# Second layer with its shared partial sum copied from PSUM to PSUM, and the weight splits of the first layer queued later

## The chip, the cores and the metric

One core of a Trainium2 chip runs the whole program. The metric is the device time of the program in microseconds. The kernel before takes 1782.92 us (median of 3 runs, 1781.92 to 1786.9).

## The reference

An attention with keys and values pooled by 8 feeds two layers, each a pair of matrix products over 4608 tokens with a model width of 512 and an inner width of 2048, all in fp32:

```python
def _moe2_ref(x, w_in, w_out):          # the second layer
    h = x @ w_in                        # 4608x512 @ 512x2048
    g = h - np.tanh(h)
    return g @ w_out                    # 4608x2048 @ 2048x512
```

The first layer has the same shape, with `g = ((clip(h, -1, 1) + 1) / 2) ** 2` joined to `h` above 1 in the place of `h - tanh(h)`.

## The kernel before

**The first layer** (lines 572 to 861) goes over 12 blocks of 384 tokens, and in each over 16 slices of the inner width: one *step* is the 12 matmuls of `h_mm`, the 12 of `out_mm` of two steps before, and the elementwise work between them. A dictionary `plan` says what else each step issues. Its slot "ev" holds the copies of the attention's PSUM tiles (`at_evac`, `kv_k_evac`), its slot "w" the preparation of the second layer's weights, one slice `f` in eight steps: `w2_conv` rebuilds fp32 numbers (lines 158 to 165), `w2_sums` forms four sums on POOL (243 to 251), `w2_own` and `w2_mixed` split each number into a high and a low part (`w2_halves`: line 254 on ACT, line 255 on DVE) and send them to DRAM (`w2_place`, line 260, from SP's queue). In this layer the order of an engine's instructions isn't that of the text: a scheduler places them by when it expects their inputs. A block `tc.issue_after(i)` adds that what it holds comes after instruction `i` on that engine.

**The second layer** (lines 868 to 1212) does each 2x2 block product with 7 products instead of 8 (Winograd's form). Tokens go in five groups `J` of 768, 1024, 1024, 1024 and 768; `half(J)` is 384 or 512. For each pair of 128-wide inner slices `q` (8 for each J, 40 in all) there are 7 `h_prod`, each of 6 matmuls of 128 x `half`, onto three PSUM banks A, X and Z. For two pairs together, `k = q // 2` (20 in all), there are 7 `o_prod` of 24 (or 18) matmuls of 256 columns, onto two PSUM tiles of two banks, bo0 and bo1. PE's order is written out by hand: two `h_prod`, one `o_prod`, and so on, with the `o_prod` eight places behind; the first 20 `h_prod` and the last `o_prod` stand alone. All engines run in the order of due times that a planner gives (`at_time`), so a late instruction holds up everything behind it on its engine.

The products share sums. Product 1 is in all four blocks of h, products 1 + 6 are in three. Before the change this is done outside PSUM: ACT copies product 1 out (`v_s`), DVE adds it to bank X after products 6, 5 and 3 (`v_w`, `v_t`, `v_c12`), DVE adds two more (`v_c22`, in SBUF, and `v_c21`), and ACT copies c11 out. Two tanh of 128 x 2 x half on ACT (`v_th`) read these blocks in SBUF, and two subtractions follow (`v_sub`), one on DVE and one on POOL. POOL then forms the sums for the second product (`g_s1` to `g_s4`), ACT and DVE split each operand into high and low (`sp_hi`, `sp_lo`), and after each `o_prod` its PSUM tile is added into one of six sums in SBUF (`add_up`), which `fold` joins on POOL at the end of a J.

At the end of a J the next group's x is loaded, split into 7 operands (`xc_hi` on ACT, `xc_lo` on DVE), with four differences between them on POOL (`x_t1` to `x_t4`). This stretch is called a *switch* below; there are four.

Of the kernel before, what the change touches and what calls it, by code (L numbers as in the profile page):

```python
# [51 lines left out]
def attention_two_moe_kernel(  # L52
# [767 lines left out]
    for f in range(FC):  # L820
# [44 lines left out]
    for x in (ps_a, ps_h, ps_o):  # L865
# [11 lines left out]
        "q0 q1 q2 q3 q4 r3 p1664 o0 o1 g0 s0 q7 q8 p2048 x1 x6 r4 o2 o3 q5 q6 g1 k0 k1 th s1 p1024"  # L877
        " r0 r1 r2 z0 p1728 aS aX a11 a12 a21 a22 u1 u2 x7 x2 x5 x4 x3"
# [5 lines left out]
    for x, n in (("bo0", 2), ("bo1", 2), ("bA", 1), ("bX", 1), ("bZ", 1)):  # L884
        TAGS[x] = one_pool(f"two_{x}", space=PSUM, reuse_waits="tile")
# [4 lines left out]
    HORD = (1, 6, 7, 2, 5, 4, 3)  # L890
# [13 lines left out]
    def wo_load(i):  # L904
        k, m = divmod(i, 7)
        t = WO2[i] = two(f"o{i % NO}", [P, 2, 2, 256], F32R, "wo")
        nc.sync.dma_start(out=t.bitcast(F32), in_=w2o[k % NGR][:, OSLOT[OORD[m]]])
# [17 lines left out]

    def xc_tile(J, m):
        x = two(f"x{m}", [P, 2, 2, M2], F32R, "xc")
        XC[(J, m)] = x[:, :, :, 0 : half(J)]
# [29 lines left out]

    def h_prod(i):
        q, mi = divmod(i, 7)  # L960
        m, J = HORD[mi], q // NPR
        bank = {1: "A", 2: "A", 6: "X", 5: "X", 3: "X", 7: "Z", 4: "Z"}[m]
        new = m in (1, 6, 7)
        if new:
            BK[(q, bank)] = two(f"b{bank}", [P, M2], F32, f"bk{bank}")[:, 0 : half(J)]
        o, x, w = BK[(q, bank)], XC[(J, m)], WQ.pop(i).rearrange("p h (c f) -> p h c f", f=P)
# [8 lines left out]
    def g_of(q, i, th=None):  # L975
# [3 lines left out]
        n2 = half(k // NGR)  # L979
        return GR[k][:, p, i, :, 0:n2] if th is None else GR[k][:, p, i, th, 0:n2]  # L980

    def snap(q, name, bank):
        s = SN[(q, name)] = two(name, [P, M2], F32, name)[:, 0 : half(q // NPR)]
        nc.scalar.activation(s, BK[(q, bank)], AF.Copy)

    def v_s(q):
        snap(q, f"s{q % 2}", "A")
# [4 lines left out]
    def s_of(q):  # L992
        return SN[(q, f"s{q % 2}")]

    def v_c11(q):
        nc.scalar.activation(g_of(q, 0, 0), BK.pop((q, "A")), AF.Copy)

    def v_w(q):
        nc.vector.tensor_tensor(g_of(q, 1, 0), BK[(q, "X")], s_of(q), ALU.add)

    def v_t(q):
        nc.vector.tensor_tensor(g_of(q, 1, 1), BK[(q, "X")], s_of(q), ALU.add)  # L1002

    def v_c22(q):
        o = g_of(q, 1, 1)
        nc.vector.tensor_tensor(o, o, SN.pop((q, "z0")), ALU.add)  # L1006

    def v_c21(q):
        o = g_of(q, 1, 0)
        nc.vector.tensor_tensor(o, BK.pop((q, "Z")), o, ALU.add)  # L1010

    def v_c12(q):
        nc.vector.tensor_tensor(g_of(q, 0, 1), BK.pop((q, "X")), SN.pop((q, f"s{q % 2}")), ALU.add)  # L1013

    def v_th(q, i):
# [46 lines left out]

    def o_prod(n):
        k, mi = divmod(n, 7)
        m, n2 = OORD[mi], half(k // NGR)
        new = m in (1, 6, 7)
        chain = {1: 0, 2: 0, 7: 1, 4: 1, 6: 2, 5: 2, 3: 2}[m]
        if new:
            OB[(k, chain)] = two(f"bo{(k + (chain == 2)) % 2}", [P, 4, 256], F32, "ob")
        o, x, w = OB[(k, chain)], SP2.pop(n), WO2.pop(n)  # L1070
        nch = n2 // P
# [19 lines left out]

    def add_up(n):
        k, mi = divmod(n, 7)
        m, J, g = OORD[mi], k // NGR, k % NGR
        name = {1: "S", 2: "11", 6: "X", 5: "22", 3: "12", 7: "22", 4: "21"}[m]
        chain = {1: 0, 2: 0, 7: 1, 4: 1, 6: 2, 5: 2, 3: 2}[m]
        o = OB[(k, chain)][:, 0 : half(J) // P]
        a = ac_of(J, name)
        if g == 0 and m != 7:
# [3 lines left out]
        if g == NGR - 1:  # L1103
            if m == 2:
                y_out(J, 0, 0, "11")
            if m == 7:
                y_out(J, 1, 1, "22")
            if m == 3:
                y_out(J, 0, 1, "12")
            if m == 4:  # L1110
                y_out(J, 1, 0, "21")

    def fold(J, name, by):
        a = ac_of(J, name)
        nc.gpsimd.tensor_tensor(a, a, ac_of(J, by), ALU.add)
# [32 lines left out]
    seq += late_o[3:] + [("o", n) for n in range(7 * NG - LAG, 7 * NG)]  # L1148
# [13 lines left out]
    for n in range(7 * NG):  # L1162
        at_time((-26, -25, -54, -0.5)[n] if n < NO else began[n - NO] + 3, wo_load, n)
        k, mi = divmod(n, 7)
        r = half(k // NGR) / M2
        t = max(began[n] - 6.6 * r, split_at(n))
        at_time(t, sp_hi, n)
        at_time(t + 1.1 * r, sp_lo, n)
    for q in range(2 * NG):
        e = {m: ended[7 * q + i] for i, m in enumerate(HORD)}  # L1170
        at_time(e[1] + 0.05, v_s, q)
        at_time(e[6] + 0.1, v_w, q)
        at_time(e[7] + 0.05, v_z, q)
# [70 lines left out]
```

## Time and profile before

| | |
|---|---|
| median of 3 runs | 1782.92 us |
| the profiled execution | 1787.46 us |
| its span, first to last instruction | 1785.6 us |
| PE busy in the span | 1699.8 us (95%) |
| DVE, ACT, POOL busy | 1214.3, 880.1, 695.2 us |
| first matmul of the second layer | at 1002.43 us of the span |
| mean granted TensorE clock | 0.986 of full speed |

The profile counts an engine as busy from an instruction's start to its end. Matmuls overlap, so a product of six matmuls is best read from the start of one product to the start of the next. "Idle before, releaser" is the time for which an engine had nothing running, and the instruction whose end let it go on. [...]

### The profile page before, as it was taken

Reading aid. Unit: us, or ns where it says so; the run is one execution under the profiler, and the core shown is the slowest. Engines: PE = TensorE matmul, PEld = TensorE weight load, DVE = VectorE, ACT = ScalarE, POOL = GpSimd, SP = SyncE. Lnnn points to the kernel's source line nnn. Section 1 sums busy time; section 2 is a strip of 40 time slices with the busy share of each in tenths; the row PEclk is TensorE's granted clock in tenths of the full one; section 3 lists DMA queues with packets and bytes.
Section 4 is the critical chain, followed back from the end, with each engine's and each line's share of the span. In section 5 each row is a group of like instructions: output and inputs, shape, how many; then the busy total and the mean of one; then the engine's idle time right before and its main releaser. Section 6 shows DMA issues by size and latency. Waiting matters only on the chain. (4 is left out here: it accounts for less than half of the span.)

```text
span 1785.6 us, 28158 instructions
## 1 busy us (share of the span) xinstructions
PE 1699.8 (95%) x10176; PEld 1586.3 (89%) x10176; DVE 1214.3 (68%) x1685; ACT 880.1 (49%) x1962; POOL 695.2 (39%) x585
## 2 busy tenths in 40 slices
PE   7999999999999999999999999899999989998996
PEld 6569989899999999998999998799889978998996
DVE  7876676666666566765545558857975797578676
ACT  5656665556555565555444354343434434433442
POOL 5441243321443223431000245543663465456342
PEclk9999999999999999999999999999999999998999
DMA  7641144424433343433111577577556756664864
GB/s 221 231 135 30 56 126 117 154 61 126 134 106 121 89 130 88 145 98 98 28 66 54 171 244 264 165 224 231 161 185 205 234 165 206 198 210 153 280 214 138
DMA packets 220218, 270.56 MB, mean 152 GB/s; under 512 B 82672, under 2 KB 151792, under 8 KB 220080
## 3 DMA queue, kind: packets, MB, share of 16 engines
q1 hardware_dynamic: 219824, 267.98, 48.3%
q8 instruction: 81, 1.33, 0.3%
q0 software_dynamic: 256, 0.79, 0.1%
q14 instruction: 57, 0.47, 0.1%
HBM read 219.94 MB, written 48.23 MB: 150 GB/s over the span
## 5 line engine op out<-in xcount | busy, mean ns | idle before, releaser
L1078 PEld LDWEIGHTS ob<-wo,sp 128*128 128x128 f32 x3024 | 385.8, 194 | 35.8 <-DVE sp L1061 17.7
L1078 PE MATMUL ob<-wo,sp 128*128 128x256 f32 x3024 | 392.5, 286 | 25.0 <-DVE sp L1061 15.7
L602 ACT ACTIVATE g<-g,half 128x384 f32<-128x384 f32 x192 | 118.7, 618 | 183.5 <-DVE g L598 181.6
L591 PE MATMUL ph<-xh,whl 128*128 128x384 f32 x704 | 197.0, 340 | 0.6 <-DVE g L606 0.6
L636 PE MATMUL po<-gh,whl 128*128 128x384 f32 x704 | 196.6, 340 | 0.0
L1021 POOL TENSOR_TENSOR g<-g,th 128x1024 f32<-128x1024 f32 (+1 forms) x40 | 90.8, 2271 | 260.2 <-ACT th L1017 168.7
L970 PE MATMUL bkX<-xc,wq 128*128 128x512 f32 (+1 forms) x720 | 175.9, 380 | 15.9 <-DVE g L1013 11.1
L479 POOL TENSOR_TENSOR ex<-ex,rc 128x432 f32<-128x432 f32 x44 | 41.7, 948 | 350.9 <-ACT g L602 176.8
L1017 ACT ACTIVATE th<-g 128x1024 f32<-128x1024 f32 (+1 forms) x80 | 78.0, 975 | 201.9 <-DVE g L1010 116.7
L1061 DVE TENSOR_TENSOR sp<-g,sp 128x1024 fp32r<-128x1024 f32 (+1 forms) x100 | 149.5, 1495 | 30.5 <-ACT sp L1056 30.4
L615 DVE TENSOR_TENSOR gl<-g,gh 128x384 fp32r<-128x384 f32 x176 | 109.1, 620 | 88.3 <-ACT gh L614 87.3
L970 PEld LDWEIGHTS bkX<-xc,wq 128*128 128x128 f32 x720 | 131.1, 192 | 35.2 <-DVE g L1013 12.6
L606 DVE TENSOR_TENSOR g<-ph,g 128x384 f32<-128x384 f32 x192 | 106.6, 555 | 65.3 <-ACT g L602 63.3
L598 DVE TENSOR_SCALAR g<-ph 128x384 f32<-128x384 f32 x192 | 105.6, 550 | 57.3 <-PE ph L591 51.9
L1102 DVE TENSOR_TENSOR ac<-ob,ac 128x1024 f32<-128x1024 f32 (+1 forms) x110 | 122.0, 1110 | 31.0 <-PE ob L1078 30.8
L1056 ACT ACTIVATE sp<-g 128x1024 fp32r<-128x1024 f32 (+1 forms) x100 | 97.0, 970 | 81.3 <-PE ob L1078 52.0
L614 ACT ACTIVATE gh<-g 128x384 fp32r<-128x384 f32 x176 | 91.8, 522 | 89.4 <-DVE g L606 51.8
L591 PEld LDWEIGHTS ph<-xh,whl 128*128 128x128 f32 x704 | 128.5, 188 | 1.9 <-DVE g L606 1.6
L636 PEld LDWEIGHTS po<-gh,whl 128*128 128x128 f32 x704 | 128.7, 188 | 0.0
L636 PE MATMUL po<-gh,wh 128*128 128x384 f32 x352 | 122.3, 347 | 0.0
L591 PE MATMUL ph<-xh,wh 128*128 128x384 f32 x352 | 121.2, 344 | 0.2 <-DVE g L606 0.2
L328 POOL TENSOR_TENSOR kvraw<-kvraw 128x768 f32<-128x768 f32 (+2 forms) x84 | 111.1, 1322 | 23.0 <-DMA kvraw<-in_v_dram 16.4
(175 smaller groups left out, 3895.7 us busy)
## 6 DMA issues: line engine op xcount, KB each, us to landing
wq<-w2c SPq DMA_DIRECT2D x280, 256.0 KB, 3.6
wo<-w2o SPq DMA_DIRECT2D x140, 512.0 KB, 3.6
wraw<-in_moe_w_in_dram SPq DMA_DIRECT2D x32, 512.0 KB, 3.9
wraw<-in_moe_w_out_dram SPq DMA_DIRECT2D x32, 512.0 KB, 5.0
out_dram<-ac SPq DMA_DIRECT2D x72, 128.0 KB, 1.8
x2d<-ost SPq DMA_DIRECT2D x44, 192.0 KB, 1.9
w2c<-wraw SPq DMA_DIRECT2D x16, 512.0 KB, 2.8
w2o<-wraw SPq DMA_DIRECT2D x16, 512.0 KB, 2.8
```

Of the source, the lines that this page charges most:

```text
L328: eng.tensor_tensor(a[..., 0:n], a[..., 0:n], a[..., n : 2 * n], ALU.add)
L591: nc.tensor.matmul(ps, a[:, cs], x[:, c, :], start=(i == 0), stop=(i == 3 * KC - 1))
L598: nc.vector.tensor_scalar(a, hp[t], -1.0, 1.0, ALU.max, ALU.min)
L602: nc.scalar.activation(a, a, AF.Square, bias=half, scale=0.5)
L606: nc.vector.tensor_tensor(a, hp.pop(t), a, ALU.max)
L615: nc.vector.tensor_tensor(gl, a, gh.bitcast(F32), ALU.subtract)
L636: nc.tensor.matmul(o, a, m, start=(f == 0 and i == 0), stop=(f == FC - 1 and i == len(ops) - 1))
L970: nc.tensor.matmul(o, w[:, wi, c], x[:, xi, c], start=new and n == 0, stop=n == 5, skip_group_check=not new)
L1056: nc.scalar.activation(x[:, 0, :, 0 : half(k // NGR)], o_src(k, OORD[mi]), AF.Copy)
L1061: nc.vector.tensor_tensor(x[:, 1], o_src(k, OORD[mi]), x[:, 0].bitcast(F32), ALU.subtract)
L1078: nc.tensor.matmul(o[:, c], x[:, xi, p, c * P : (c + 1) * P], w[:, p, wi], start=new and first, stop=True, skip_group_check=not (new and f ...
L1102: nc.vector.tensor_tensor(a, o, a, ALU.add)
```

## The change

In the first layer, `w2_sums` is issued one step earlier, and `w2_own` and `w2_mixed` go through `behind`, which puts their ACT and DVE instructions after the newest one of the text on the same engine.

In the second layer, ACT copies product 1 from bank A into bank X (`v_seed`), and products 6, 5 and 3 accumulate onto it there. ACT takes one copy of 1 + 6 out of X (`v_u`), and DVE writes c21 in place in bank Z and c22 into a new bank Y, the second half of a tile that it shares with A. The four tanh read PSUM, one block each, and the four subtractions are all on DVE, from PSUM into SBUF. `o_prod` does likewise: ACT copies product 1's tile into the tile of products 6, 5 and 3 (`o_seed`), so four output sums remain, and `fold` is gone. `open_x` and `fill` are a few matmuls that open a bank ahead of the first copy into it. Products 6 and 7 change places. The operands of x rotate through eight buffers instead of seven, and their due times move forward. The last eight `o_prod` change their order.

```diff
+    def behind(fn, *a):
+        with tc.issue_after(newest(E.Activation)), tc.issue_after(newest(E.DVE)):
+            fn(*a)
...
-        add(t + 4, "w", w2_sums, f)
-        add(t + 5, "w", w2_own, f)
-        add(t + 6, "w", w2_mixed, f)
+        add(t + 3, "w", w2_sums, f)
+        add(t + 5, "w", behind, w2_own, f)
+        add(t + 6, "w", behind, w2_mixed, f)
...
-    for x, n in (("bo0", 2), ("bo1", 2), ("bA", 1), ("bX", 1), ("bZ", 1)):
+    for x, n in (("bo0", 2), ("bo1", 2), ("bA", 2), ("bX", 1), ("bZ", 1)):
...
-    HORD = (1, 6, 7, 2, 5, 4, 3)
+    HORD = (1, 7, 6, 2, 5, 4, 3)
...
+    def fill(o, w):
+        for i in range(0, o.shape[1], M2):
+            nc.tensor.matmul(o[:, i : i + M2], w[:, 0:P], w, start=True, stop=True)
...
+    def v_seed(q):
+        nc.scalar.activation(new_bank(q, "X"), bank(q, "A"), AF.Copy)
...
-    def v_w(q):
-        nc.vector.tensor_tensor(g_of(q, 1, 0), BK[(q, "X")], s_of(q), ALU.add)
-
-    def v_t(q):
-        nc.vector.tensor_tensor(g_of(q, 1, 1), BK[(q, "X")], s_of(q), ALU.add)
+    def v_u(q):
+        snap(q, f"s{q % 2}", "X")
 
     def v_c22(q):
-        o = g_of(q, 1, 1)
-        nc.vector.tensor_tensor(o, o, SN.pop((q, "z0")), ALU.add)
+        nc.vector.tensor_tensor(bank(q, "Y"), bank(q, "X"), SN.pop((q, "z0")), ALU.add)
...
+    def v_c21(q):
+        o = bank(q, "Z")
+        nc.vector.tensor_tensor(o, o, SN.pop((q, f"s{q % 2}")), ALU.add)
...
+    def v_th(q, b):
+        th = SN[(q, b)] = two(f"t{next(n_th) % 2}", [P, M2], F32, "th")[:, 0 : half(q // NPR)]
+        nc.scalar.activation(th, bank(q, b), AF.Tanh)
+
+    def v_sub(q, b):
+        nc.vector.tensor_tensor(g_of(q, *WHERE[b]), BK.pop((q, b)), SN.pop((q, b)), ALU.subtract)
...
+    def o_seed(k):
+        o = OB[(k, 2)] = two(chain_bank(k, 2), [P, 4, 256], F32, "ob")
+        c = half(k // NGR) // P
+        nc.scalar.activation(o[:, 0:c], OB[(k, 0)][:, 0:c], AF.Copy)
...
-        if g == 0 and m != 7:
+        if g == 0 and m not in (7, 4):
             nc.scalar.activation(a, o, AF.Copy)
         else:
             nc.vector.tensor_tensor(a, o, a, ALU.add)
...
-    def fold(J, name, by):
-        a = ac_of(J, name)
-        nc.gpsimd.tensor_tensor(a, a, ac_of(J, by), ALU.add)
...
-    seq += late_o[3:] + [("o", n) for n in range(7 * NG - LAG, 7 * NG)]
+    end = [("o", n) for n in range(7 * NG - LAG, 7 * NG)]
+    seq += late_o[3:] + [end[i] for i in (1, 0, 3, 2, 5, 4, 7, 6)]
...
+        at_time(e[1] + 0.05, v_seed, q)
         at_time(e[7] + 0.05, v_z, q)
+        at_time(e[6] + 0.05, v_u, q)
+        at_time(e[2] + 0.1, v_th, q, "A")
+        at_time(e[2] + 0.9, v_sub, q, "A")
+        at_time(e[5] + 0.05, v_c22, q)
+        at_time(e[5] + 0.9, v_th, q, "Y")
+        at_time(e[5] + 1.6, v_sub, q, "Y")
         at_time(e[4] + 0.05, v_c21, q)
+        at_time(e[4] + 0.9, v_th, q, "Z")
+        at_time(e[4] + 1.6, v_sub, q, "Z")
+        at_time(e[3] + 0.05, v_th, q, "X")
+        at_time(e[3] + 0.8, v_sub, q, "X")
...
-        lo = {1: 2.6, 6: 10.6, 2: 12.6, 7: 15.6, 5: 21.6, 4: 25.6, 3: 29.6}
...
+                t = max(free, min(ended[last] + (-8, 4, 8, 10.5, 15, 19, 23)[i], due))
```

`e[m]` is the planned end of product `m` of pair `q`, and `ended[last]` that of the first product of a J's last pair.

## Rows read from the trace of the kernel before

**Rows 1.** Windows of layer two: stretch, length, busy PE PEld DVE ACT POOL, clock, DMA.

```profile
1100.00:1155.00 55.00, 44.64 (x259) 38.47 (x258) 48.85 (x41) 21.19 (x27) 31.86 (x13) 0.97 0.55 168
1155.00:1265.00 110.00, 110.00 (x697) 99.52 (x697) 74.06 (x67) 47.42 (x54) 55.29 (x20) 1.00 0.70 221
1265.00:1325.00 60.00, 51.76 (x307) 45.81 (x307) 51.77 (x40) 23.57 (x27) 35.04 (x13) 0.94 0.51 153
...
1435.00:1490.00 55.00, 46.70 (x275) 41.28 (x274) 47.25 (x35) 21.46 (x25) 35.79 (x13) 0.94 0.52 158
...
1615.00:1670.00 55.00, 48.30 (x319) 47.69 (x318) 45.19 (x37) 19.32 (x26) 36.85 (x14) 0.91 0.58 190
...
1742.00:1785.60 43.60, 30.14 (x223) 28.72 (x222) 28.71 (x31) 9.91 (x12) 11.10 (x5) 0.96 0.44 133
```

**Rows 2.** Waits of PE in 1000:1790: total us, times, longest us.

```profile
PE ob L1078 <- DVE sp L1061: 15.7, 10, 2.7
PE bkX L970 <- DVE g L1013: 11.1, 5, 4.4
```

**Rows 3.** Timeline of DVE around the second switch: start, us, instruction.

```profile
1283.84 2.83 DVE L1061 TENSOR_TENSOR sp<-g,sp 128x1024 fp32r<-128x1024 f32 x1
...
1301.89 3.41 DVE L1021 TENSOR_TENSOR g<-g,th 128x1024 f32<-128x1024 f32 x1
...
1318.01 1.22 DVE L1061 TENSOR_TENSOR sp<-g,sp 128x1024 fp32r<-128x1024 f32 x1
```

**Rows 4.** Timeline of POOL over the same stretch.

```profile
1282.31 3.27 POOL L1035 TENSOR_TENSOR u<-g 128x1024 f32<-128x1024 f32 x1
...
1295.69 8.52 POOL L1115 TENSOR_TENSOR ac<-ac 128x1024 f32<-128x1024 f32 x3 [3.43 <-DVE ac L1102]
```

**Rows 5.** Three lines of DVE, whole run: duration ns min/median/max, first and last start.

```profile
L1006 DVE TENSOR_TENSOR g<-g,z x40: 551/684/2760, 1008.5 to 1742.5; 128x512 f32<-128x512 f32 x24, 128x384 f32<-128x384 f32 x16
...
L1013 DVE TENSOR_TENSOR g<-bkX,s x40: 543/678/693, 1010.0 to 1743.4; 128x512 f32<-128x512 f32 x24, 128x384 f32<-128x384 f32 x16
...
L1102 DVE TENSOR_TENSOR ac<-ob,ac x110: 943/1211/1225, 1043.7 to 1780.8; 128x1024 f32<-128x1024 f32 x66, 128x768 f32<-128x768 f32 x44
```

**Rows 6.** The same for ACT's copy out of bank Z.

```profile
L984 ACT ACTIVATE z<-bkZ x40: 472/598/602, 1005.8 to 1736.8; 128x512 f32<-128x512 f32 x24, 128x384 f32<-128x384 f32 x16
```

**Rows 7.** Windows of layer one, two stretches and the sum over 240:1000.

```profile
495.00:600.00 105.00, 97.83 (x573) 93.81 (x572) 66.06 (x119) 57.67 (x169) 41.06 (x61) 0.98 0.42 127
...
735.00:840.00 105.00, 99.34 (x566) 95.53 (x565) 66.76 (x121) 58.33 (x169) 39.06 (x55) 0.95 0.36 109
...
sum 760.00, PE 737.86 PEld 722.22 DVE 468.32 ACT 411.70 POOL 210.66; mean PE 73.79 PEld 72.22 DVE 46.83 ACT 41.17 POOL 21.07
```

**Rows 8.** Waits of PE in 240:840.

```profile
PE psc L450 <- ACT kt L377: 7.1, 7, 2.0
PE ppv L548 <- DVE al L530: 6.5, 5, 2.6
PE ppv L551 <- DVE al L530: 3.9, 3, 1.3
```

**Rows 9.** Timelines of ACT and of DVE around one weight split, 255:268.

```profile
258.96 1.06 ACT L254 ACTIVATE wraw<-wf 128x1024 fp32r<-128x1024 f32 x1 [0.44 <-DVE wf L165]
...
261.87 1.23 DVE L255 TENSOR_TENSOR wf<-wf,wraw 128x1024 fp32r<-128x1024 f32 x1 [2.13 <-POOL wraw L246]
```

**Rows 10.** Timeline of PE around the second switch and in the last stretch.

```profile
1277.95 3.04 PE L1078 MATMUL ob<-wo,sp 128*128 128x256 f32 x24
1280.83 1.57 PE L970 MATMUL bkZ<-xc,wq 128*128 128x512 f32 x6
1282.24 1.56 PE L970 MATMUL bkA<-xc,wq 128*128 128x512 f32 x6
...
1749.09 2.39 PE L1078 MATMUL ob<-wo,sp 128*128 128x256 f32 x18 [1.60 <-ACT th L1017]
```

**Rows 11.** ACT's wait for the next slice's weights, whole run.

```profile
ACT wraw L158 <- DMA wraw<-in_moe_w_out_dram: 13.9, 10, 3.8
```

More of the change, by code (lines that the diff above doesn't have):

```diff
@@ L957, in x_t4, with bank, new_bank @@
         x_eng(J).tensor_tensor(XR[(J, 1)], XR[(J, 1)], x_src(J, 6), ALU.subtract)
+    BANK = {1: "A", 2: "A", 6: "X", 5: "X", 3: "X", 7: "Z", 4: "Z"}
+    def bank(q, b):
+        return BK[(q, b)]
+    def new_bank(q, b):
+        if b == "A":
+            t = two("bA", [P, 4, 256], F32, "bkA").rearrange("p c f -> p (c f)")
+            BK[(q, "Y")] = t[:, M2 : M2 + half(q // NPR)]
+        else:
+            t = two(f"b{b}", [P, M2], F32, f"bk{b}")
+        o = BK[(q, b)] = t[:, 0 : half(q // NPR)]
+        return o
     def h_prod(i):
@@ L961, in h_prod @@
         m, J = HORD[mi], q // NPR
[L962 to L966, printed above, removed]
+        new = m in (1, 7)
+        o = new_bank(q, BANK[m]) if new else bank(q, BANK[m])
+        x, w = XC[(J, m)], WQ.pop(i).rearrange("p h (c f) -> p h c f", f=P)
         n = 0
@@ L973, in h_prod, with open_x, g_of @@
                 n += 1
-    def g_of(q, i, th=None):
+    def fill(o, w):
+        for i in range(0, o.shape[1], M2):
+            nc.tensor.matmul(o[:, i : i + M2], w[:, 0:P], w, start=True, stop=True)
+    def open_x():
+        fill(two("bX", [P, M2], F32, "bkX"), WQ[0].rearrange("p h f -> p (h f)"))
+    def g_of(q, i, th):
         k, p = divmod(q, 2)
@@ L1061, in sp_lo, with chain_bank @@
         nc.vector.tensor_tensor(x[:, 1], o_src(k, OORD[mi]), x[:, 0].bitcast(F32), ALU.subtract)
+    W1 = {}
+    CHAIN = {1: 0, 2: 0, 7: 1, 4: 1, 6: 2, 5: 2, 3: 2}
+    def chain_bank(k, chain):
+        if k == NG - 1 and chain == 0:
+            return "bA"
+        return f"bo{(k + (chain == 2) + (k == NG - 1)) % 2}"
     def o_prod(n):
@@ L1065, in o_prod @@
         m, n2 = OORD[mi], half(k // NGR)
-        new = m in (1, 6, 7)
-        chain = {1: 0, 2: 0, 7: 1, 4: 1, 6: 2, 5: 2, 3: 2}[m]
+        new, chain = m in (1, 7), CHAIN[m]
         if new:
-            OB[(k, chain)] = two(f"bo{(k + (chain == 2)) % 2}", [P, 4, 256], F32, "ob")
+            OB[(k, chain)] = two(chain_bank(k, chain), [P, 4, 256], F32, "ob")
         o, x, w = OB[(k, chain)], SP2.pop(n), WO2.pop(n)
+        if m == 1:
+            W1[k] = w
         nch = n2 // P
@@ L1094, in add_up @@
         m, J, g = OORD[mi], k // NGR, k % NGR
-        name = {1: "S", 2: "11", 6: "X", 5: "22", 3: "12", 7: "22", 4: "21"}[m]
-        chain = {1: 0, 2: 0, 7: 1, 4: 1, 6: 2, 5: 2, 3: 2}[m]
-        o = OB[(k, chain)][:, 0 : half(J) // P]
+        if m == 1:
+            if k in (0, NGR):
+                b = two(chain_bank(k, 2), [P, 4, 256], F32, "ob").rearrange("p c f -> p (c f)")
+                fill(b, W1.pop(k)[:, 0].rearrange("p h f -> p (h f)"))
+            o_seed(k)
+            return
+        name = {2: "11", 6: "21", 5: "22", 3: "12", 7: "22", 4: "21"}[m]
+        o = OB[(k, CHAIN[m])][:, 0 : half(J) // P]
         a = ac_of(J, name)
-        if g == 0 and m != 7:
+        if g == 0 and m not in (7, 4):
             nc.scalar.activation(a, o, AF.Copy)
@@ L1102, in add_up @@
             nc.vector.tensor_tensor(a, o, a, ALU.add)
[L1103 to L1111, printed above, removed]
-    def fold(J, name, by):
-        a = ac_of(J, name)
-        nc.gpsimd.tensor_tensor(a, a, ac_of(J, by), ALU.add)
+        if g == NGR - 1 and m in (2, 5 if k == NG - 1 else 7, 3, 4):
+            y_out(J, int(name[0]) - 1, int(name[1]) - 1, name)
     def y_out(J, th, dh, name):
@@ L1147, in attention_two_moe_kernel @@
         seq.insert(len(seq) - 10 + 4 * i - i, x)
-    seq += late_o[3:] + [("o", n) for n in range(7 * NG - LAG, 7 * NG)]
+    end = [("o", n) for n in range(7 * NG - LAG, 7 * NG)]
+    seq += late_o[3:] + [end[i] for i in (1, 0, 3, 2, 5, 4, 7, 6)]
+    ordo = [i for kind, i in seq if kind == "o"]
+    POS = {n: i for i, n in enumerate(ordo)}
     for kind, i in seq:
```

73 lines of the change are left out of this document (27 added, 46 removed).

## The prediction, made before any run of the changed kernel

> **What bounds the kernel now.** I read the windows by stretch first, then PE's waits, then the timelines around them. In layer two PE is busy without a gap between the switches (110.00 of 110.00 us in 1155:1265 [rows 1]), so there no other engine's saving is worth anything. What can be saved lies in five places. [...] The last stretch has 13.5 us without PE, of which about 5 lie behind the last product (the last sum starts at 1780.8 [rows 5], and then its DMA), and 0.04 of 43.6 us by the clock: 8.6 + 1.7 = 10.3 us.
>
> What PE waits for there is DVE: 15.7 us for the low halves of `o_prod`'s operands, and 11.1 us for the sum (`v_c12`) that frees bank X [rows 2]. At the switches DVE is busy 48.9 of 55, 51.8 of 60, 47.3 of 55 and 45.2 of 55 us; between them, 74.1 of 110 [rows 1]. Part of this isn't work. A low half takes 1.22 us alone, but 2.83 us while POOL's `g_s1` runs beside it; DVE's subtraction took 3.41 us beside POOL's folds and what followed them [rows 3, 4]. The sum in SBUF, `v_c22`, has a median of 684 ns and a longest of 2760; the sums with one input in PSUM never go over 693 (512 columns) and 1225 (1024) [rows 5], although POOL ran beside many of them. So an addition of two SBUF tensors slows down beside POOL, one with a PSUM input doesn't.
>
> In layer one PE idles 22.1 us between 240 and 1000 [rows 7], and 17.5 us of its waits are for the attention's copies out of PSUM, `kt` and `al` [rows 8]; the clock of 0.98 and 0.95 in two stretches of 105 us adds 7.4 us [rows 7]. The timeline shows how: a weight split's high half (1.06 us) stands ahead of the copies on ACT, and its low half stands on DVE for 2.13 us until POOL has finished `w2_sums`, which read what it overwrites [rows 9].
>
> **The change, part by part.** *DVE at a switch.* For each pair, five sums of 0.69 us and a subtraction of 1.22 (this is L1102's median as well [rows 5]) become two sums and four subtractions of 0.69 us, all with a PSUM input: 4.67 becomes 4.14 us, and a switch of some 50 us holds 2.5 pairs, 1.3 us. The sum of product 1 (1.21 us [rows 5]) goes once in such a stretch. The first split of x moves from 2.6 us behind the switch to 8 us ahead of it, 1.2 us by [rows 3]'s alone value. POOL loses a subtraction for each pair and four folds for each J; three folds alone took 8.52 us [rows 4], so with the fourth and two or three subtractions about 17 of its 35 busy us [rows 1] are gone. The excess of DVE's instructions with two SBUF inputs over their lone times is what goes with it. In [rows 3] it is 1.6 us for the low half and 2.2 for the subtraction; `v_c22` and the subtraction also leave the kind that is slowed. Taking 2.2 us for the subtraction, 2.1 for one `v_c22` (its longest less its median), and half of 1.6 for each of four low halves gives 7.5 us. DVE gains about 1.3 + 1.2 + 1.2 + 7.5 = 11 us where PE idles 6.7 to 10.4. The relief is as large as the stall, so I expect most of it gone, and with the gaps the stretches at half clock. What is late next is the first low half behind the switch: it stands behind two splits of x while `g_s1` and `g_s2` run, and has some 2 us to spare. I keep 9 of 47.1 us for that: **-38 us**. Bounds: -47 (nothing left) and -24 (half: if the contention with `g_s1` to `g_s4` and `x_t1` to `x_t4`, which stay, is the larger part).
>
> *New waits of PE.* Four chains now pass through two or three engines before a bank is free. For A and Y: `v_c22`, tanh, subtraction, then product 1 of the next pair. Three instructions at 0.69, 0.60 [rows 6] and 0.69, and an allowance of 0.1 for each hand-over, are 2.3 us. Behind product 5 stand products 4 and 3, 1.41 us each, and always an `o_prod` of 2.88 [rows 10]: 5.7 us. X (tanh, subtraction, `v_seed`) and Z have the same 5.7, and `v_seed` itself (0.6 to 0.9 us; the trace shows no write to PSUM but PE's, the copy in [rows 6] is nearest and I take its 0.6) has product 7 and an `o_prod`, 4.3 us. All are covered by about 3.4 us of slack while DVE isn't late: cost nothing. Behind a waiting seed ACT would hold the next `sp_hi`, and PE the rest of its list. At the start of layer two no `o_prod` lies between: two products at three quarters of 1.41 us give 2.1 us against 0.75 of 2.3 plus `v_c21` ahead in DVE's queue, about 2.2. I take 0.3 us for each of two or three pairs, and under 1 us for the few matmuls of `fill`: **+1.5 us** (0 to 4).
>
> `o_seed` has two `h_prod` of cover (2.8 us for a copy of about 1.1), and in the tail the new order puts two other `o_prod` between. PE gets no more matmuls elsewhere. ACT has seven copies and tanh of 0.6 us for a pair in the place of three and two of twice the size, 0.1 to 0.4 us more; it is busy 47.4 of 110 us in the steady stretch [rows 1], so that is hidden.
>
> In this trace a 512-column sum costs DVE the same from PSUM as from SBUF, 678 and 684 ns in the median [rows 5]. [...]
>
> *The tail.* The first stall there waits for a tanh ahead of POOL's subtraction [rows 10]. Now the subtractions are on DVE block by block, so product 1's operand is ready before the last `h_prod` ends; the folds, beside which low halves were slow, are gone; one sum less is made. But `sp_hi` of a product still waits for the buffer of the second one before, with DVE's `g_s1` to `g_s4` in the queue: about a fifth of a product late at several places. **-5.5 us** of 10.3 (-2 to -8).
>
> *Weight splits.* High and low halves now follow the copies of the attention, and `w2_sums`, a step earlier, are done before. The waits of 17.5 us [rows 8] less one of 2.0 in which ACT stood at a weight load, and the 7.4 us of clock, are 22.9 us at stake. The 32 splits still take 1.06 and 1.23 us each on ACT and DVE, only elsewhere, so I take a bit over half: **-13 us** (0 to -22). What the later place costs: SP's `w2_place` moves with it, and so does the load of the next slice into the same buffer, for which ACT already waits 13.9 us [rows 11].
>
> **The sum.** -38 + 1.5 - 5.5 - 13 = -55 us. The profiled execution took 1787.46 us (span 1785.6 and 1.9 around it), 4.5 over the median; 1787.5 - 55 is 1732.5 for such an execution, and 1782.9 - 55 = **1728 us** for the median.
>
> **The rivals.** *All of it* (0.13): every gap at the switches goes, 8 us in the tail, 22 in layer one: -77, 1706 us. For it: 11 us of relief against 6.7 to 10.4.
> *Half* (0.18): DVE is still the later one at the switches (-24), the splits only move the stall (0), tail -2, start +3: -23, 1760 us. For it: `g_s1` to `g_s4` stay on POOL and meet the splits of x.
> *The next weights come late* (0.05): with mixed splits in their planned step, the load has two steps; ACT stands at line 158 as in its longest waits, 2 us for each of 15 slices, all passed on to PE: +30 for -13, so -12, 1771 us. Against it: layer two's weights are complete long before they are read.
> *Slower: the bank chain* (0.06). At product 1 of a pair PE waits for `v_c22`, tanh and subtraction if DVE's queue is more than 3.4 us late in ordinary stretches; each us beyond that costs 40 us over 40 pairs. With 1.8 us beyond (72 us) against -55, 1800 us; it decides from 1.4 us on. For it: waits for the same kind of sum reach 4.4 us at the switches [rows 2]. Against it: between them PE never waits, with a DVE two thirds busy.
> *It doesn't act* (0.03): PE's waits are set by something that the profile names wrongly, such as the weights' DMA; then within 0.3% of 1783.
>
> **How the numbers follow.** The forecast (0.55, some 14 us to either side by its bounds) is 1728. The range has to hold 8 in 10: it goes a little past the middle of the first rival to 1702, and past that of the second to 1766, so that it takes in about three quarters of each (0.10 and 0.14) beside the forecast, 0.79. A measurement of this kernel can tell about 0.3%, 5 us. Faster by more: 0.55 + 0.13 + 0.18 + 0.05 = 0.91; within: 0.03; slower: 0.06.
>
> **What would show it.** Right: in the windows around the four switches PE idles under 3 us each at a clock of 0.98 or more; POOL's busy time falls by over 100 us, with 40 subtractions and 20 folds gone; DVE's subtractions take 0.7 us and the low halves are rarely over 2 us; `kt` and `al` cost PE under 8 us. Wrong: PE's waits name bank A or X behind a subtraction or a seed away from the switches, or ACT's wait for the weights grows; or the switches keep their gaps although DVE is free, in which case another queue set them.

## The result, and the profile after

| | before | after |
|---|---|---|
| median, same chip | 1784.91 us (4 runs, 1781.92 to 1787.47) | 1714.34 us (4 runs, 1711.2 to 1715.59) |
| ratio | | 0.9603, 95% interval 0.958 to 0.9625 |
| span of the profiled execution | 1785.6 us | 1709.3 us |
| first matmul onto bank A (end of layer one) | 1002.4 | 982.2 |
| first to last matmul onto bank A | 737.3 | 686.5 |
| from there to the end of the span | 45.9 | 40.6 |

The change saves 70.6 us by the medians and 76.3 by the two profiled spans, of which 20.2 lie in layer one, 50.8 between the first and the last matmul onto bank A (this stretch holds the four switches), and 5.3 in the tail. The profiled execution of before is the longest of its four and that of after the shortest, which is why the spans give more than the medians; part of the 20.2 is that (see the experiments). The three stretches come from two rows: the span, and the first and last start of the matmuls onto A. After (profile of that tile; duration min/median/max in ns, then first and last start):

```profile
core 0 of [0], span 1709.3 us
...
L992 PE MATMUL bkA<-xc,wq x480: 331/392/499, 982.2 to 1668.7; 128*128 128x512 f32 x96, 128*128 128x384 f32 x64
```

The page of after, busy time, share of the span and instructions: POOL is 155 us less busy than the 695.2 of before, DVE 89 less, ACT 9 more, and PE is busy 98% of the span.

```profile
PE 1673.2 (98%) x10181; PEld 1571.8 (92%) x10181; DVE 1125.5 (66%) x1675; ACT 889.2 (52%) x2052; POOL 539.8 (32%) x525
```

Windows of after at the four switches, each beginning 2 to 5 us ahead of the first low half of the new x (columns as in [rows 1]), and their sum. Against the 10.4, 8.2, 8.3 and 6.7 us of [rows 1], PE idles 0.5 us in the first and nothing in the others, and the granted clock is 1.00 in all four.

```profile
1060.00:1115.00 55.00, 54.54 (x355) 51.07 (x354) 44.27 (x49) 29.28 (x45) 23.04 (x10) 1.00 0.75 234
1205.00:1265.00 60.00, 60.00 (x378) 53.88 (x377) 50.21 (x44) 31.14 (x42) 27.13 (x10) 1.00 0.60 180
1365.00:1420.00 55.00, 55.00 (x352) 49.62 (x351) 47.70 (x43) 29.57 (x39) 25.62 (x10) 1.00 0.64 191
1525.00:1580.00 55.00, 55.00 (x379) 52.37 (x378) 42.69 (x44) 27.98 (x41) 22.73 (x9) 1.00 0.63 193
sum 225.00, PE 224.54 PEld 206.94 DVE 184.88 ACT 117.97 POOL 98.53; mean PE 56.13 PEld 51.74 DVE 46.22 ACT 29.49 POOL 24.63
```

The same four stretches of before, begun 6 to 10 us ahead of the same low half, in sum. PE idles 31.4 us of 225 (one gap of 2.2 us at the third switch lies behind the window; [rows 1] has 33.6). The thing to keep for later is that DVE is busy 208.6.

```profile
sum 225.00, PE 193.65 PEld 175.02 DVE 208.60 ACT 91.12 POOL 152.21; mean PE 48.41 PEld 43.75 DVE 52.15 ACT 22.78 POOL 38.05
```

Over the whole stretch from the first to the last matmul onto A, PE's idle time falls from 36.4 to 0.5 us, and its busy time for the same matmuls from 700.9 to 686.0, at a mean granted clock of 0.98 before and 1.00 after (before, it is 0.50 in 1287:1290, right behind a gap of 2.69 us; after, it is 1.00 at every switch). These are the 50.8 us: 35.9 and 14.9.

[rows 2] leaves out what PE waited for at the first switch of before. In 1090:1145 it is mostly the splits of x, 6.4 us of 10.4:

```profile
PE bkZ L970 <- DVE xc L941: 3.5, 2, 2.0
PE bkX L970 <- DVE xc L941: 2.3, 1, 2.3
...
PE bkZ L970 <- ACT xc L937: 0.6, 1, 0.6
```

PE's waits of after in 1000:1710 (total, times, longest). They answer to [rows 2]: nothing waits for a sum that frees a bank, and low halves cost 0.5 us in the place of 15.7 (once, at the first switch). The other four lines are waits in the tail.

```profile
PE ob L1104 <- ACT ob L1121: 1.6, 1, 1.6
PE ob L1104 <- ACT sp L1073: 1.6, 1, 1.6
PE ob L1104 <- DMA wo<-w2o: 1.1, 1, 1.1
PE ob L1104 <- issue: 0.9, 2, 0.7
PE ob L1104 <- DVE sp L1078: 0.5, 1, 0.5
```

The new instructions, whole run (L1024 is `v_c22`, L1038 a subtraction, L1011 `v_seed`, L1035 a tanh; they answer to [rows 5, 6]): each takes what the prediction gave it, 0.58 to 0.70 us.

```profile
L1024 DVE TENSOR_TENSOR bkA<-bkX,z x40: 566/699/700, 988.0 to 1670.4; 128x512 f32<-128x512 f32 x24, 128x384 f32<-128x384 f32 x16
...
L1038 DVE TENSOR_TENSOR g<-bkA,th x80: 541/679/693, 987.3 to 1672.2; 128x512 f32<-128x512 f32 x48, 128x384 f32<-128x384 f32 x32
...
L1011 ACT ACTIVATE bkX<-bkA x40: 475/582/592, 983.4 to 1663.8; 128x512 f32<-128x512 f32 x24, 128x384 f32<-128x384 f32 x16
...
L1035 ACT ACTIVATE th<-bkA x80: 478/597/601, 986.8 to 1671.0; 128x512 f32<-128x512 f32 x48, 128x384 f32<-128x384 f32 x32
```

PE's waits of after in layer one, 240:840. Of [rows 8] the `al` waits (10.4 us) are gone. `kt` costs as much as before, and a wait for POOL's `rr` has grown.

```profile
PE psc L454 <- ACT kt L381: 8.0, 5, 3.2
PE par L510 <- POOL rr L492: 5.7, 5, 1.7
```

### The profile page after: what moved, and what is told of

The parts are those of the page before. It is cut to its first block, busy times and chain, and to the rows that moved or that the text cites. A ratio compares the mean times of both kernels' runs of the same rounds, so it can differ in the third digit from the quotient of the medians.

```text
span 1709.3 us, 28221 instructions
## 1 busy us (share of the span) xinstructions
PE 1673.2 (98%) x10181; PEld 1571.8 (92%) x10181; DVE 1125.5 (66%) x1675; ACT 889.2 (52%) x2052; POOL 539.8 (32%) x525
## 5 line engine op out<-in xcount | busy, mean ns | idle before, releaser
L1104 PEld LDWEIGHTS ob<-wo,sp 128*128 128x128 f32 x3024 | 378.7, 191 | 14.3 <-ACT sp L1073 3.0
L1104 PE MATMUL ob<-wo,sp 128*128 128x256 f32 x3024 | 383.7, 283 | 5.6 <-ACT ob L1121 1.6
L619 DVE TENSOR_TENSOR gl<-g,gh 128x384 fp32r<-128x384 f32 x176 | 128.9, 732 | 98.9 <-ACT gh L618 98.3
L1078 DVE TENSOR_TENSOR sp<-g,sp 128x1024 fp32r<-128x1024 f32 (+1 forms) x100 | 133.2, 1332 | 81.5 <-ACT sp L1073 81.4
L992 PE MATMUL bkX<-xc,wq 128*128 128x512 f32 (+1 forms) x720 | 170.4, 371 | 0.0
L1138 DVE TENSOR_TENSOR ac<-ob,ac 128x1024 f32<-128x1024 f32 (+1 forms) x100 | 111.3, 1113 | 49.7 <-PE ob L1104 49.3
L1052 POOL TENSOR_TENSOR u<-g 128x1024 f32<-128x1024 f32 (+1 forms) x19 | 44.9, 2364 | 290.5 <-DVE g L1038 290.5
L595 PE MATMUL ph<-xl,whl 128*128 128x384 f32 x352 | 118.7, 337 | 0.0
L595 PE MATMUL ph<-xh,wl 128*128 128x384 f32 x352 | 118.5, 337 | 0.0
```

What stands on the lines that cost most here:

```text
L595: nc.tensor.matmul(ps, a[:, cs], x[:, c, :], start=(i == 0), stop=(i == 3 * KC - 1))
L619: nc.vector.tensor_tensor(gl, a, gh.bitcast(F32), ALU.subtract)
L992: nc.tensor.matmul(o, w[:, wi, c], x[:, xi, c], start=new and n == 0, stop=n == 5, skip_group_check=not new)
L1078: nc.vector.tensor_tensor(x[:, 1], o_src(k, OORD[mi]), x[:, 0].bitcast(F32), ALU.subtract)
L1104: nc.tensor.matmul(o[:, c], x[:, xi, p, c * P : (c + 1) * P], w[:, p, wi], start=new and first, stop=True, skip_group_check=not (new and f ...
L1138: nc.vector.tensor_tensor(a, o, a, ALU.add)
```

## The experiments

The prediction laid the switches to DVE: 11 us of its work there would go, most of that time lost beside POOL. The experiments ask whether it was DVE's amount of work, POOL's company, or something else. The table gives the stretches of every run as above (layer one, first to last matmul onto A, tail), in us of its profiled execution; the medians are in the text. Layer one has the same code in eight of these kernels (after, e1, e4 to e7, e11, e12) and takes 982.2 to 992.1 there, so the middle column tells more of layer two than a median does. That column repeats well: after, e8 and e10 share their second layer and have 686.5, 686.5 and 686.7, before and e1 737.3 and 738.5.

Much of layer one's spread arises at its beginning. The second layer's weights are begun behind the 385th of the 2240 recorded matmuls onto the tile `ph`; up to there the code is that of every other kernel here, and yet it ends anywhere from 231.5 to 240.2 us; the first matmul onto `ph` already starts anywhere from 35.3 to 43.4.

| kernel | layer one | first to last on A | tail |
|---|---|---|---|
| before | 1002.4 | 737.3 | 45.9 |
| after | 982.2 | 686.5 | 40.6 |
| before, POOL's subtraction and folds left out (e14) | 1001.3 | 695.3 | 43.2 |
| the same, POOL as busy off the path (e15) | 1005.4 | 712.4 | 48.0 |
| before, only the folds left out (e17) | 1000.3 | 716.7 | 44.6 |
| after, POOL as busy off the path (e5) | 982.2 | 688.8 | 40.8 |
| after, a POOL step on the path (e11) | 986.8 | 689.1 | 41.2 |
| after, subtractions twice (e6) | 992.1 | 700.1 | 43.9 |
| after, old x handling (e4) | 986.1 | 698.5 | 40.2 |
| after, e4 and e5 together (e12) | 987.3 | 706.9 | 41.7 |
| after, old order of the end (e7) | 987.6 | 686.6 | 41.6 |
| before, layer one's part alone (e1) | 985.0 | 738.5 | 46.1 |
| after, weight conversion queued behind too (e8) | 976.8 | 686.5 | 40.5 |
| the same, `w2_sums` a step later again (e10) | 983.1 | 686.7 | 41.2 |

### Put POOL back beside DVE (e5)

```diff
+            nc.gpsimd.tensor_tensor(o, g_of(q, 0, 1), o, ALU.add)
...
+            nc.gpsimd.tensor_tensor(o, o, o, ALU.add)
```

The first line runs twice for each pair, the second eight times for each J at the due times of the folds; `o` is a spare tile.

> The kernel after with POOL as busy as before: for each pair two additions of half a block beside the place of the old subtraction, and for each J eight of them at the due times of the old folds, on a spare buffer; nothing waits for their results but POOL's own queue. Mine (an addition of two SBUF tensors on DVE slows down beside POOL): low halves near a switch over 2 us again, PE idle at the four switches 12 us or more together, 1730 to 1750 us. Rivals (fewer DVE instructions, or the earlier splits of x, decide): under 5 us more, at most 1720 us.

Measured: 1716.58 us (1713.52 to 1717.91), 2 us over after, where the rivals had it and I had 1730 or more; the stretch on A is 2.3 longer. The low halves did become slow: those of u have a median of 1835 ns in this run (1706 in before), against 1224 in after. Rows of this run and of after:

```profile
L1091 DVE TENSOR_TENSOR sp<-u,sp x40: 941/1835/2353, 1008.0 to 1696.9; 128x1024 fp32r<-128x1024 f32 x24, 128x768 fp32r<-128x768 f32 x16
```

```profile
L1078 DVE TENSOR_TENSOR sp<-u,sp x40: 941/1224/2870, 1007.8 to 1694.6; 128x1024 fp32r<-128x1024 f32 x24, 128x768 fp32r<-128x768 f32 x16
```

So the contention is real, but in the changed kernel it costs no more than 2.3 us. As the one decisive cause it falls.

### Give DVE its work back (e6)

```diff
-        nc.vector.tensor_tensor(g_of(q, *WHERE[b]), BK.pop((q, b)), SN.pop((q, b)), ALU.subtract)
+        x, th = BK.pop((q, b)), SN.pop((q, b))
+        for _ in (0, 1):
+            nc.vector.tensor_tensor(g_of(q, *WHERE[b]), x, th, ALU.subtract)
```

> The kernel after with each of the four subtractions of a pair done twice, the same result written again: DVE gets about 2.4 us more for a pair, 6 us at a switch, without more work on POOL. Mine: DVE near its limit at the switches only, 3 to 15 us, 1717 to 1730 us, and no wait between the switches, since the chains that free the banks have about 3.4 us of slack. Rival (the number of DVE instructions decides, not the contention): 1735 us or more. The bank chain, my slower case: PE waits for a subtraction or a seed between the switches too, 40 us or more.

Measured: 1734.59 us (1726.25 to 1737.84); the stretch on A is 13.6 longer, about a quarter of the 50.8. The windows of its four switches in sum:

```profile
sum 225.00, PE 219.34 PEld 200.04 DVE 210.81 ACT 114.15 POOL 100.84; mean PE 54.84 PEld 50.01 DVE 52.70 ACT 28.54 POOL 25.21
```

DVE is as busy here as in before (210.8 and 208.6 us), and PE idles 5.7 us, not 31.4. So a DVE this busy doesn't make the gaps by itself; that it had no part in them in the kernel before isn't shown, since this run starts from the kernel after. The median lies between the two expectations. By the profiled spans this run is 26.8 us longer than after: besides the 13.6, which are in my range of 3 to 15, there are 9.9 in layer one, which this edit doesn't touch (6.4 of them arise at its beginning), and 3.3 in the tail. Between the switches PE waits for nothing, as I had expected.

### Take POOL out of the kernel before (e14), and keep it busy off the path (e15)

e14 leaves out `fold` and POOL's half of `v_sub`; e15 adds to it the additions of e5:

```diff
-        eng = nc.vector if i else nc.gpsimd
-        eng.tensor_tensor(g_of(q, i), g_of(q, i), SN.pop((q, i)), ALU.subtract)
+        th = SN.pop((q, i))
+        if i:
+            nc.vector.tensor_tensor(g_of(q, i), g_of(q, i), th, ALU.subtract)
...
-            at_time(began[o] + 4.5 + 2.7 * i, fold, J, name, by)
-        at_time(began[o + 1] + 9, fold, J, "21", "X")
+            pass
```

> The kernel before, without the folds of the output sums and without POOL's subtraction h - tanh(h) for the blocks c11 and c12: the kernel leaves these parts of the computation out, all else stays, the sums in PSUM and SBUF by DVE, the x times and the banks too. It removes POOL's company for DVE and POOL's step in the path at the same time. If POOL (by contention or by its place in the path) set the gaps at the switches: 25 to 45 us less than the kernel before, 1740 to 1760. If the gaps come from DVE's own work, from the order in which bank X comes free, or from the late splits of x: 0 to 12 us less, 1773 to 1785.

> The kernel before, again without the folds and without POOL's subtraction for c11 and c12 (these parts of the computation are left out), but with POOL additions of the same number and size in their place, whose result nobody reads: beside the output sums as the folds stood, and behind g_s1 to g_s4 instead of ahead of them. Without any such work the kernel took 1740, 44 us less than the kernel before. Theory 'contention' (DVE's additions of two SBUF tensors slow down beside POOL, and that set the gaps at the switches): most of the 44 us comes back, 1765 to 1785. Theory 'path' (POOL's subtraction of about 3 us, behind folds that wait for DVE, held g_s1 to g_s4 and so the low halves of the output operands): nearly nothing comes back, 1738 to 1748. In between: both, in that proportion.

Measured: e14 1740.17 us (1738.55 to 1744.44), 43.7 under the 1783.84 of before beside it; e15 1759.04 (1757.42 to 1767.59), 29.2 under the 1788.19 of before beside it, so 14.5 of the 43.7 came back (18.9 by the two medians alone). The stretch on A lies between: 737.3, then 695.3 without this work of POOL, then 712.4, so 17.1 back. e14 is where the theory that POOL set the gaps had it, e15 between its two theories. The windows of the four switches, e14 first:

```profile
sum 225.00, PE 217.99 PEld 199.48 DVE 193.78 ACT 103.04 POOL 97.92; mean PE 54.50 PEld 49.87 DVE 48.44 ACT 25.76 POOL 24.48
```

```profile
sum 225.00, PE 206.97 PEld 186.87 DVE 200.27 ACT 98.91 POOL 180.16; mean PE 51.74 PEld 46.72 DVE 50.07 ACT 24.73 POOL 45.04
```

Taking two things from POOL, with before's sums, banks and x as they were, removes 42.0 of the 50.8 us. PE's idle time in these windows falls from 31.4 to 7.0 us; with POOL busy again, off the path, it is 18.0. So POOL's work is the cause of most of the gaps in the kernel before, and company placed as in e15, where POOL is busier than in before (180.2 and 152.2 us), is worth 17 of the 42. The other 25 go by difference to its place: in the chain, or beside just those DVE instructions that can't wait. No run separates these two, but the second switch of before shows both. Its first gap, in the timelines of ACT, POOL and PE (start, us, instruction, idle before it and its releaser; the low half between is the first of [rows 3]):

```profile
1278.69 1.06 ACT L1017 ACTIVATE th<-g 128x1024 f32<-128x1024 f32 x1 [3.70 <-DVE g L1021]
...
1282.27 1.06 ACT L1056 ACTIVATE sp<-g 128x1024 fp32r<-128x1024 f32 x1 [1.08 <-POOL g L1021]
```

```profile
1279.83 2.40 POOL L1021 TENSOR_TENSOR g<-g,th 128x1024 f32<-128x1024 f32 x1 [5.13 <-DVE ac L1102]
```

```profile
1286.72 4.40 PE L1078 MATMUL ob<-wo,sp 128*128 128x256 f32 x22 [2.69 <-DVE sp L1061]
```

The second tanh starts only when DVE's subtraction has freed the one `th` buffer (1278.69); it ends at 1279.75 and POOL's subtraction begins (the releaser named, `ac`, ended at the same moment), 2.40 us; then the high half, and the low half, held by `g_s1`, until 1286.67; then PE. That is a chain, with 2.4 us of POOL in it and 1.6 of company. The next two gaps are company: DVE's timeline beside the three folds of [rows 4] (1295.69 to 1304.21), with the subtraction of [rows 3] right behind, and PE's:

```profile
1296.25 2.39 DVE L1006 TENSOR_TENSOR g<-g,z 128x512 f32<-128x512 f32 x1
...
1299.16 2.80 DVE L1061 TENSOR_TENSOR sp<-g,sp 128x1024 fp32r<-128x1024 f32 x1
```

```profile
1302.02 2.90 PE L1078 MATMUL ob<-wo,sp 128*128 128x256 f32 x22 [2.20 <-DVE sp L1061]
...
1307.08 2.79 PE L970 MATMUL bkX<-xc,wq 128*128 128x512 f32 x6 [2.17 <-DVE g L1013]
```

`v_c22`, the low half and the subtraction are held 1.7, 1.6 and 2.2 us one after the other, by the kind of delay that the prediction priced, and PE waits for what stands behind them.

### The folds alone (e17)

```diff
-            at_time(began[o] + 4.5 + 2.7 * i, fold, J, name, by)
-        at_time(began[o + 1] + 9, fold, J, "21", "X")
+            pass
```

> The kernel before without the folds alone (the output sums stay unjoined, a part of the computation left out); POOL's subtraction stays in its place on the path. If the folds were what held POOL's queue at the switches (each waits for DVE's output sum, 3.4 us, and takes 1.8 to 2.9 us): 25 to 44 us less than the kernel before, 1740 to 1760. If the subtraction's own time is what counts: 0 to 15 us less, 1769 to 1784.

Measured: 1763.8 us (1759.94 to 1765.38), 24.4 under the 1788.19 of before beside it (20.6 on A). So about half of POOL's 42.0 us is the folds', and by difference half the subtraction's; the time lies between the two expectations.

### POOL back on the path of the changed kernel (e11)

```diff
+    def through_pool(q):
+        for i in (0, 1):
+            o = g_of(q, 0, i)
+            nc.gpsimd.tensor_tensor(o, o, PAD["p2048"][:, 0 : half(q // NPR)], ALU.add)
...
+        at_time(e[3] + 2.0, through_pool, q)
```

> The changed kernel, with one step added: behind the subtractions of a pair, POOL adds a tile of zeros to the two g blocks c11 and c12 (two additions of up to 512 columns from SBUF), so that POOL stands again between the subtraction and the sums g_s1 to g_s4, and between it and the high half of the first output product, as in the kernel before. The values stay as they are. The run with POOL kept busy beside DVE, but off the path, cost only 2 us against the changed kernel's 1714. Theory 'path': the gaps at the four switches came from POOL's place in the chain from tanh to the operands (a subtraction of about 3 us behind folds in POOL's queue) and from PE's waits for low halves behind it; then most of the 47 us at the switches comes back, 30 to 45 us, 1744 to 1760. Theory 'several reliefs': each relief alone is larger than the stall, so taking one back costs little: 1715 to 1722. Between the two, some gaps of 1 to 3 us only at the switches: 1722 to 1735.

Measured: 1715.19 us (1712.87 to 1718.88), 2.6 us more on A, as "several reliefs" had it. The theory "path" as written falls too. The changed kernel has slack that takes up POOL's step as it takes up its company.

### The x handling alone, and with POOL's company (e4, e12)

e4 takes back the eighth buffer and the due times of `xc_hi` and `xc_lo`; e12 has the edits of e4 and e5.

```diff
-        x = two(f"x{XTAG[(J, m)]}", [P, 2, 2, M2], F32R, "xc")
+        x = two(f"x{m}", [P, 2, 2, M2], F32R, "xc")
...
-                t = max(free, min(ended[last] + (-8, 4, 8, 10.5, 15, 19, 23)[i], due))
+            t = max(e[m] + 1.2, min(e[1] + d, due)) if J else e[m] + 1.2 + (6 if m in (6, 7, 4) else 0)
```

> The kernel after with the old handling of x at a switch: seven buffers, and the due times of before (first split 2.6 us behind the switch instead of 8 ahead). Mine (the gaps went because DVE is relieved of POOL's company and of instructions): 1715 to 1724 us, PE idle at the four switches under 8 us together. Rival (the earlier splits and the eighth buffer did it): 1735 us or more, with PE waiting for xc and for low halves at the switches as before, some 20 us together.

> The changed kernel with two reliefs taken back at once: x has its seven buffers and its old due times again (alone: +12 us), and POOL has additions of the kind and number that the change took from it, off the path (alone: +2 us). The added POOL work changes nothing of the output. Theory 'several reliefs' (my contention theory in a weaker form: DVE has so much slack at the switches that one loss is absorbed, two are not): clearly more than the sum of the two, 1740 to 1760. If the two only add up, 1726 to 1732, contention with POOL has little to do with the gaps at the switches even when DVE's slack is used up, and the cause lies in the banks or in the path from tanh to the operands.

Measured: e4 1726.72 us (1724.59 to 1727.08), e12 1737.86 (1735.22 to 1738.7). On A: e5 +2.3, e4 +12.0, both +20.4. e4 lies between its two expectations, with PE idle 5.4 us in its four windows, most of it (3.9 us) in one wait for a split of x at the first switch:

```profile
PE bkZ L988 <- DVE xc L947: 3.9, 1, 3.9
```

The windows of e12's switches:

```profile
sum 225.00, PE 212.23 PEld 192.23 DVE 193.42 ACT 105.66 POOL 172.34; mean PE 53.06 PEld 48.06 DVE 48.35 ACT 26.42 POOL 43.09
```

With x split late, POOL's company costs 8.4 us where it cost 2.3 with x split early. That is between the two expectations, nearer to "several reliefs": the early x is part of the slack that makes the rest cheap. But both together bring back only two fifths of the 50.8.

### The end's order (e7)

```diff
...
-    seq += late_o[3:] + [end[i] for i in (1, 0, 3, 2, 5, 4, 7, 6)]
+    seq += late_o[3:] + end
...
```

> The kernel after with the last eight products of the second matrix in their old order, so that product 6 stands right behind product 1, whose sum is copied for it. Mine: the copy of 0.8 us and what stands ahead of it are exposed once, 1 to 3 us more in the last stretch, 1715 to 1718 us. Rival (the order is what shortened the tail): 5 us more or over.

Measured: 1716.35 us (1712.9 to 1717.66), as expected; tail 41.6 and 40.6. Five kernels with the end of after (e4, e5, e8, e10, e11) have tails of 40.2 to 41.2, so the order itself is worth about 1 us at most, and that isn't clear of the spread. The rest of the tail's 5.3 comes with the other parts (e14, without POOL's work, has 2.7 of it).

### Layer one's part alone (e1), and further along the same way (e8, e10)

e1 is the kernel before with `behind` and `w2_sums` a step earlier. e8 is the changed kernel with one more pair of steps queued behind; e10 also moves `w2_sums` back.

```diff
-        add(t, "w", w2_conv, f, 0)
-        add(t + 2, "w", w2_conv, f, 1)
+        add(t, "w", behind, w2_conv, f, 0)
+        add(t + 2, "w", behind, w2_conv, f, 1)
...
-        add(t + 3, "w", w2_sums, f)
+        add(t + 4, "w", w2_sums, f)
```

> The kernel before with the first layer's part of the change alone: the sums for the second layer's weights one step earlier, the splits queued behind. The prediction gave it 13 us (1772); the excess of PE's issue times between the traces of before and after in layer one gives 20 us (1765). If it is worth nothing by itself and layer one's gain came from something of layer two: 1783 to 1788.

> The changed kernel with w2_conv also queued behind the newest instructions of ACT and DVE. In the changed kernel ACT stands three times at its first instruction, which waits for the next weights' DMA, with the attention's copy kt behind it, and PE idles 2.2, 3.2 and 2.2 us there. If that is all of it: those 7.6 us and the half clock that follows go, 1703 to 1710. If the conversion then comes too late and passes the wait on to the splits and the next load: 1714 to 1722. Nothing either way: 1711 to 1716.

> The same with w2_sums back in its old step, since in the changed kernel PE waits 5.7 us for a reciprocal that stands behind w2_sums and the attention's work in POOL's queue. If both readings hold: 1698 to 1706. If the low halves wait for the sums again, now with nothing of the attention behind them: as without this, 1703 to 1710. If the later sums hold the splits and, by them, the next load: 1714 to 1725.

Measured: e1 1770.22 us (1766.67 to 1771.42), 13.6 under before (ratio 0.9918 [0.9885, 0.995]) and between its two expectations; layer one ends at 985.0 in the place of 1002.4, and layer two is as before. Behind the 385th matmul onto `ph` layer one takes 765.4 to 770.2 us in the four kernels without this edit (before, e14, e15, e17) and 748.4 to 753.1 in the eight with it: 16 us by the means. e8 1706.65 (1705.57 to 1712.89), ratio to before 0.9555 [0.9534, 0.9576], the quickest version here, with layer one at 976.8, and in the first of its expectations; e10 1712.27 (1706.44 to 1712.76), in none of its own. But e8 didn't do it as I read the trace. That reading, in ACT's timeline of after:

```profile
538.21 0.65 ACT L158 ACTIVATE wraw<-wraw 128x512 int32<-128x512 uint32 x1 [2.87 <-DMA wraw<-in_moe_w_in_dram]
538.76 0.27 ACT L381 ACTIVATE kt<-pkt 128x144 f32<-128x144 f32 x1
```

`kt` stands behind an instruction that waits for weights; this and two more such places make 7.6 of the 8.0 us. PE's waits of e8 in 240:840:

```profile
PE psc L454 <- ACT kt L381: 8.4, 5, 2.9
PE ppv L554 <- ACT ar L527: 1.2, 3, 0.6
```

The `kt` waits are no smaller. ACT's timeline of e8 says why: the first conversion still stands ahead of `kt`, here as at the other two places, so this edit didn't put the reading to the test:

```profile
532.80 0.67 ACT L158 ACTIVATE wraw<-wraw 128x512 int32<-128x512 uint32 x1 [2.53 <-DMA wraw<-in_moe_w_in_dram]
533.38 0.26 ACT L381 ACTIVATE kt<-pkt 128x144 f32<-128x144 f32 x1
```

The `rr` waits, which I laid to `w2_sums`, are gone without its being moved. Of the 5.4 us by which the trace of e8 is ahead of that of after in layer one, 2.3 arise at the beginning that all kernels share; of the 6.3 by which e10 is behind e8, 4.0. What is left, 3.1 and 2.3 us, is less than the spread of that part among the eight kernels above (4.7), though e8's 745.3 lies below all eight. Why e8 is quicker than after, and whether e10 is slower than e8 for a reason, stays open.

## Why the prediction was right, step by step

*Where the time lay.* Right. The stretches between the switches were without a gap before and are now; the gain is in the four switches and the tail, 50.8 + 5.3 us in layer two, and 20.2 in layer one. With the 16 us of e1's section for layer one the three make 72, close to the 70.6 of the medians.

*DVE at a switch (-38 of 47, with +1.5 for the new waits).* The 47.1 us are the 33.6 in which PE idles in the four stretches of [rows 1] and 13.5 for what the granted clock lacks there of 1.00, times the stretches' lengths. That second part was the author's estimate, which no run shows by itself; in its place the two traces show PE busy 14.9 us less for the same matmuls. The -38 was too small, and the reasoning behind it holds only in part. The stretch on A fell by 50.8 us, beyond the bound of 47: that is the rival "all of it" for layer two, and 2.3 us of idle time at the layer's start are gone as well. The 9 us kept for the first low half behind the splits of x don't appear (0.5 us at the first switch). The step that failed is the one that turned relief into gain: it added up DVE's busy time, 11 us for each switch, as if any of it were worth the same. With DVE as busy as before (e6), PE idles 5.7 us of 225. That the sum came as near to the time as it did is in part luck.

What was right is the largest term, the contention: POOL is the main cause in the kernel before (42.0 us). That its 2.2, 2.1 and 1.6 us for single instructions are found again as 2.2, 1.7 and 1.6 in the second and third gap is no check of it, since the prediction had read them from the same trace, the 2.2 from this very instruction. The splits of x were given 1.2 us; PE waited 6.4 us for them at the first switch alone, and their old handling costs 12.0 in the changed kernel. What is missing is a term for the chain: POOL's own subtraction (2.4 us) and the one `th` buffer stood between tanh and PE in the first gap, and the change took both out; the prediction counted POOL's subtraction as company alone.

In the kernel after, no single part is needed: company costs 2.3 us, a POOL step in the chain 2.6, the late x 12.0, late x and company 20.4, and DVE's former work 13.6. How the 25 us divide between the chain and the moments at which the folds fell isn't settled, and which parts of the change (two `th` buffers, tanh and subtraction block by block from PSUM) give the slack that makes POOL's step free wasn't tried.

*New waits (+1.5).* None: at the start of layer two PE is busy 77.80 of 77.80 us in 982.2:1060, and behind it waits for no bank. The bank chains are covered as worked out. They show as soon as DVE is late: in e6 PE waits for banks A and Z behind subtractions, eight times in the four switches, 0.7 us at most. Between the switches e6 has none. The slower rival, which wanted them there, had its mechanism right and lacked the lateness.

*Tail (-5.5).* 5.3 measured; the wait for `o_seed` (1.6 us), which I had covered by two other products, is one of the four that remain.

*Weight splits (-13).* 13.6 by e1's median, 16 by the part of layer one that holds them; near enough. The 20.2 between the two traces is more than that because of layer one's spread. The rival "next weights come late" is there as well, small: over the whole run ACT's wait for the two kinds of weights goes from 18.3 to 23.0 us, `kt` costs PE 8.0 us, 7.6 of them behind such a wait, where I wanted all of `kt` and `al` under 8; it is nothing like 2 us for each slice.

*VectorE on PSUM.* The row held: a subtraction with a PSUM source takes 679 ns in the median, as a sum did in [rows 5] (678), and `v_c22`, which also writes to PSUM, 699.

## What to carry to other kernels

When an engine waits, ask what stands behind it in its queue (here `kt`, behind a conversion that waited 2.87 us for weights) and who waits for that, and price the whole chain; a microsecond of busy time saved on the engine that PE names is not a microsecond of gap. Where several parts of a change each relieve the same stall, taking one back tells what it is worth with the others there, so undo them from the side of the kernel before as well: POOL's part is worth 42 us there and 3 here. And read a stage by its own landmarks (the first and the last matmul onto a tile), since another stage's spread can be larger than the effect (here 9.9 us in layer one, against 2.3 for POOL's company).

## What the runs showed of the hardware

In the second layer of before, a subtraction of two SBUF tensors on DVE that begins while a POOL instruction on SBUF runs doesn't just run more slowly: as the times read, it stands still until POOL's instruction has ended, and ends 1.1 us behind it, where alone it takes 1.2 (1024 columns). In [rows 3, 4] `g_s1` ends at 1282.31 + 3.27 = 1285.58 and the low half at 1283.84 + 2.83 = 1286.67, 1.09 later. The next pair of the same stretch of before, POOL's `g_s3` (end 1292.26) and DVE's low half (end 1293.35), gives 1.09 again:

```profile
1288.87 3.39 POOL L1042 TENSOR_TENSOR g<-g 128x1024 f32<-128x1024 f32 x1
```

```profile
1290.04 3.31 DVE L1061 TENSOR_TENSOR sp<-u,sp 128x1024 fp32r<-128x1024 f32 x1
```

In that layer 90 low halves and splits of x begin beside a POOL instruction. They end 0.81 to 1.09 us behind it, with a median of 1.08 (a narrow one, of 768 columns, takes 0.94 us alone). `v_c22`, an addition of two SBUF tensors, does so seven times and ends 0.41 to 0.55 us behind it, where alone it takes 0.55 to 0.69. So the price is about what is left of POOL's instruction: the longest of the 90 took 3.31 us, 2.1 more than alone. By this a longer POOL instruction would be worse company, which no run tried. With one source in PSUM nothing of this shows: in before 60 sums of up to 512 columns begin beside a POOL instruction and take 693 ns at most, and 44 of up to 1024 columns 1225, where those that don't take up to 694 and 1225; in after no subtraction with a PSUM source goes over 693.
